# Scores and values of two heads in one matmul, by 32-key groups, in an attention and expert kernel on Trainium2

## The chip, the cores and the metric

The kernel runs on one core of a Trainium2 chip. The metric is device time in microseconds of one execution. Three runs of the kernel before took 649.19, 650.42 and 650.88 us, a median of 650.42. One more execution was taken by the hardware profiler; its own time is in the table below.

## The reference

The kernel computes a windowed attention over q, k and v (batch 8, 8 heads, 576 positions, 64 features, all float32) and feeds the result to a mixture of 8 experts. Of the reference these lines matter:

```python
rel = pos[:, None] - pos[None, :]
mask_plain = (rel >= 0) & (rel < window)
mask_dil = (rel >= 0) & (rel < window * dilation) & (rel % dilation == 0)
masks = np.stack([mask_plain if h < H // 2 else mask_dil for h in range(H)], axis=0)
scores = np.where(masks[None, :, :, :], scores, -1000000000.0)
...
e = fresh_e if s == 0 or local_gate[b, s] < 0.5 else (prev_e if prev_e >= 0 else fresh_e)
...
h = np.maximum(x[b, s] @ w1[e], 0.0)
out[b, s] = p[e] * (h @ w2[e])
```

The window is 32 and the dilation 4. With the positions of a dilated head sorted by their remainder, its mask is a window of at most 32 keys too, so each query sees at most the 32 keys up to its own, in both kinds of heads. The expert of a token is its own best one or, where a gate is open, that of the token before it; then come two matmuls with that expert's weights.

## The kernel before, in words

**Stages.** Attention runs over 32 pairs of heads (`NPB`), each with the 128 features of two heads on the 128 partitions. Its result x goes to DRAM (`xd`). While pairs are worked, the routing of finished tokens (gate logits, the carried choice, places in each expert's list) is cut into steps that run between pairs. Then come units of up to 256 tokens of one expert: rows of `xd` are gathered by index (`xg`, L959 to L960), turned, and multiplied with that expert's weights (L1088, L1183). Weights come as loads of 2 MB (L876) into `raw1` and `raw2`.

**One pair.** `scores(n)` multiplies keys by queries in nine blocks of 64 keys for each head (L342): the weights are the 64 features of one head times 64 keys, so the tile of the array is 64x64 and the two heads lie in different halves of its rows. A score tile has, for each head, 256 columns of queries (`UNITS` part 0) or 320 (part 1), so 512 or 640 columns in all; keys of even and odd blocks lie on the lower and upper 64 partitions. VectorE (DVE) applies the mask (L348: max with -640, then min with the mask), ScalarE (ACT) the exponential (L351). `values(n)` multiplies the probabilities, 64 queries at a time, by 128 keys of values with a column of ones behind them (65 columns, L404); DVE divides by the sum in that column (L408, L409) and writes x. A float32 matmul is two instructions on TensorE (PE): 20 score matmuls are 40, and 18 value matmuls are 36.

**Values in two layouts.** The 128 keys that a block of 64 queries needs begin at even blocks for one half of the queries and at odd ones for the other. The load brings one arrangement; `spread(m)` writes the other with two copies on GpSimd (POOL) for each group m of two pairs: L283 (64x1040) and L284 (64x780).

**Loads and stores.** SyncE (SP) issues all loads and stores of attention: for each m one of keys and queries (1184 KB), one of values (650 KB), and three stores of x. Three buffers of each kind rotate. A DMA of SP raises one of eight semaphores in rotation and waits for the one that was issued eight earlier.

**Order.** The orders of PE and DVE are the program's own (`manual_schedule`). The loop over n has this body: load for m = n // 2 + 2 (n even), transposes of an earlier x (`turn`), scores of n, a slot of routing (`gap`), values of n - 1, spread, more transposes and slots, the store of an earlier x. The orders of POOL, ACT and SP are set by the compiler's scheduler from its own estimates, within the dependences. The steps `early_tokens` (in a slot near n = 28) let the first units' rows be gathered: DVE clears one element of `xg` (L959), POOL issues the gather (L960). POOL also makes the table `what` of each routing group (L628), which PE needs for the sums of the group.

## Time and profile before

| what | value |
|---|---|
| median of three runs | 650.42 us |
| time of the profiled execution | 646.66 us |
| span of the profiled execution, first to last instruction | 644.9 us |
| last x of attention ends | 140.9 us |
| PE busy | 606.5 us (94%) |
| DVE busy | 417.6 us (65%) |
| ACT busy | 176.6 us (27%) |
| POOL busy | 243.6 us (38%) |
| DMA moved | 140.12 MB |

The span is what the views divide; the 1.8 us between it and the execution's time lie outside the first and last instruction. In rows of groups, the columns are line, engine, operation, tile written and tile read, shapes, count, then busy time in us and the mean of one in ns, then the idle time before these instructions with what ended it. In rows of the timeline, the first number is the start and the second the time from the start of the first to the end of the last of so many instructions.

### The profile page before, as it was taken

How to read it: one execution, taken by the hardware profiler on the slowest of the kernel's cores; microseconds unless marked ns; L12 is line 12 of the kernel's file. 1: busy time of each engine (PE TensorE's matmuls, PEld its weight loads, DVE VectorE, ACT ScalarE, POOL GpSimd, SP SyncE). 2: the span in 40 equal slices, each digit the busy share in tenths (PEclk: the TensorE clock that was granted, in tenths of full speed). 3: DMA queues.
4: the chain of work that ended last, by engine and by line, in shares of the span. 5: the costliest groups of instructions: out<-in, count | busy, mean ns of one | idle time of the engine just before them, and what ended most of it. 6: DMA issues, size and time to landing. Idle time of an engine off the chain costs nothing.

```text
span 644.9 us, 15442 instructions
## 1 busy us (share of the span) xinstructions
PE 606.5 (94%) x6350; PEld 532.4 (83%) x6350; DVE 417.6 (65%) x976; ACT 176.6 (27%) x320; POOL 243.6 (38%) x219
## 2 busy tenths in 40 slices
PE   6888988889989999999999999999999999999995
PEld 6776776768878899999598998995979999879984
DVE  3768989989596487672747487628292974473851
ACT  2545444353111232212122222121222211213210
POOL 3322142124003655464685435345544455001011
PEclk8999999999999999999999999999999999999998
DMA  9998989398004689677363665855453767470301
GB/s 346 412 326 292 346 279 299 122 363 319 2 33 156 217 321 354 227 257 250 116 238 108 245 240 205 296 188 193 168 187 151 279 229 260 147 270 37 137 33 42
DMA packets 29744, 140.12 MB, mean 217 GB/s; under 512 B 4892, under 2 KB 15260, under 8 KB 23136
## 3 DMA queue, kind: packets, MB, share of 16 engines
q1 hardware_dynamic: 22096, 119.89, 51.0%
q0 software_dynamic: 7568, 19.15, 8.6%
q8 instruction: 52, 0.85, 0.5%
q14 instruction: 28, 0.23, 0.1%
HBM read 145.31 MB, written 19.14 MB: 255 GB/s over the span
## 4 chain that ended last, share of the span: by engine, by line
PE 71%; DVE 15%; issue 6%; DMA 4%; POOL 2%; SPq 0%; ACT 0%; POOLq 0%; DVEq 0%
PE yp L1183 28%; PE hp L1088 20%; PE pv L404 3%; PE hp L1062 3%; PE yp L1171 3%; PE sc L342 3%; DVE pr L348 2%; PE tp L423 2%; DMA vt<-in_v_dram 2%; DVE x L409 1%; POOL xg L960 1%; PE hp L1049 1%; PE yp L1136 1%; PE hp L1039 1%; DMA out_dram<-y,corner 1%
## 5 line engine op out<-in xcount | busy, mean ns | idle before, releaser
L960 POOL DMA_INDIRECT xg<-xd,at x116 | 131.7, 1136 | 142.8 <-DVE xg L959 117.8
L1098 DVE TENSOR_TENSOR h<-hp,h 128x512 f32<-128x512 f32 x45 | 30.7, 688 | 97.2 <-PE hp L1088 97.2
L1183 PE MATMUL yp<-sum,hc 128*128 128x256 f32 x384 | 88.5, 380 | 0.0
L1088 PE MATMUL hp<-xc,sum 128*128 128x128 f32 x720 | 85.6, 275 | 0.0
L1124 POOL DMA_INDIRECT out_dram<-y,tok x35 | 46.9, 1341 | 96.8 <-DVE y L1198 44.7
L1088 PEld LDWEIGHTS hp<-xc,sum 128*128 128x128 f32 x720 | 82.9, 192 | 0.1
L1183 PEld LDWEIGHTS yp<-sum,hc 128*128 128x128 f32 x384 | 72.8, 190 | 9.9
L1198 DVE SCALAR_TENSOR_TENSOR y<-yp,gate,y 128x256 f32<-128x256 f32 x48 | 23.0, 483 | 63.5 <-issue 34.5
L1183 PE MATMUL yp<-raw,h 128*128 128x256 f32 x256 | 61.2, 382 | 0.0
L351 ACT ACTIVATE pr<-pr 128x512 f32<-128x512 f32 x64 | 43.8, 685 | 60.5 <-DVE pr L348 57.9
L1088 PE MATMUL hp<-xe,raw 128*128 128x128 f32 x480 | 58.9, 276 | 0.7 <-ACT xe L993 0.7
L1088 PEld LDWEIGHTS hp<-xe,raw 128*128 128x128 f32 x480 | 56.4, 192 | 1.8 <-ACT xe L993 1.0
L348 DVE SCALAR_TENSOR_TENSOR pr<-sc,mk 128x512 f32<-128x512 f32 x64 | 45.5, 748 | 15.6 <-PE sc L342 14.1
L1183 PEld LDWEIGHTS yp<-raw,h 128*128 128x128 f32 x256 | 47.4, 190 | 9.1 <-issue 3.3
L404 PE MATMUL pv<-vt,pr 128*64 128x65 f32 x1152 | 44.0, 230 | 9.0 <-issue 4.8
L404 PEld LDWEIGHTS pv<-vt,pr 128*64 128x64 f32 x1152 | 38.7, 142 | 12.2 <-issue 6.6
L1099 ACT ACTIVATE h<-h 128x512 f32<-128x512 f32 x45 | 28.4, 632 | 64.6 <-DVE h L1098 51.1
L1092 ACT COPY h<-hp 128x512 f32<-128x512 f32 x45 | 26.4, 586 | 62.4 <-PE hp L1088 62.4
L342 PE MATMUL sc<-kq 64*64 64x96 f32 (+3 forms) x1280 | 35.4, 248 | 6.7 <-issue 2.9
L342 PEld LDWEIGHTS sc<-kq 64*64 64x64 f32 x1280 | 29.5, 138 | 12.4 <-DVE pr L348 4.4
L283 POOL COPY vt<-vt 64x1040 f32<-64x1040 f32 x16 | 16.8, 1052 | 60.6 <-DMA vt<-in_v_dram 46.6
L1191 ACT ACTIVATE y<-yp,gate 128x256 f32<-128x256 f32 x48 | 22.8, 475 | 61.0 <-PE yp L1183 61.0
(248 smaller groups left out, 956.5 us busy)
## 6 DMA issues: line engine op xcount, KB each, us to landing
raw<-in_w_dram SPq DMA_DIRECT2D x50, 2048.0 KB
kq<-in_qk_dram SPq DMA_DIRECT2D x13, 1184.0 KB
vt<-in_v_dram SPq DMA_DIRECT2D x15, 650.0 KB
xd<-x SPq DMA_DIRECT2D x16, 512.0 KB
kq<-in_qk_dram SPq DMA_DIRECT2D x6, 592.0 KB
xg<-xd,at POOLq DMA_INDIRECT x116, 4.3
xd<-x SPq DMA_DIRECT2D x32, 32.0 KB
vt<-in_v_dram SPq DMA_DIRECT2D x2, 325.0 KB
```

The costliest lines, as they stand in the source:

```text
L342: nc.tensor.matmul(sc[c:c + QB, u, lo - a * QB:hi - a * QB], lhsT=kt[h, WIN + j * QB:WIN + (j + 1) * QB], rhs=qt[h, lo:hi], start=True, st ...
L348: nc.vector.scalar_tensor_tensor(to, sc[:, :, :w], -CEIL, mk[:, at:at + w].unsqueeze(1).to_broadcast([P, 2, w]), Alu.max, Alu.min)
L351: nc.scalar.activation(to, to, Act.Exp, scale=SCALE)
L404: nc.tensor.matmul(pv[half * QB:(half + 1) * QB, k - a], lhsT=pr[:, u, (i - a) * QB:(i - a + 1) * QB], rhs=vt[:, slot(i), u], start=True, ...
L960: nc.gpsimd.indirect_dma_start(out=to, out_offset=None, in_=of, in_offset=bass.IndirectOffsetOnAxis(ap=place, axis=0))
L1088: nc.tensor.matmul(to[:, m], lhsT=a[:, m, kk], rhs=b[:, kk], start=first and m == 0 and kk == 0, stop=(kk == DK // 2 - 1), skip_group_chec ...
L1092: nc.scalar.copy(at((0, 1, 3)[k]), of)
L1098: nc.vector.tensor_tensor(at(k), of, at(k), op=Alu.add)
L1099: nc.scalar.activation(at(k), at(k), Act.Relu)
L1124: nc.gpsimd.indirect_dma_start(out=rows_of_out(), out_offset=bass.IndirectOffsetOnAxis(ap=of_unit(u, "tok", j), axis=0), in_=y, in_offset= ...
L1183: nc.tensor.matmul(to, lhsT=a[:, m], rhs=b[:, m], start=first and m == 0, stop=(m == FK // 2 - 1), skip_group_check=True)
L1198: nc.vector.scalar_tensor_tensor(at(k), of, of_unit(u, "gate", k // 2), at(k), Alu.mult, Alu.add)
```

## The change

Both heads of a pair go through one matmul. Keys and values are laid out so that a column (of keys) or a row (of values) belongs to one head and holds zeros in the other head's place.

- **Scores.** Groups of 32 keys in place of 64, both heads at once: the weights are 128 features by 64 columns, 32 keys of one head and 32 of the other, with zeros at the features of the other head. The keys of a group are read with a stride of 18. Each group meets 64 queries (its own 32 and the next 32), 32 at the edges. A score tile has 256 or 320 columns, 576 for a pair in place of 1152; its partitions hold both heads. 19 matmuls a pair, in 128x64 tiles.
- **Values.** 32 queries by 128 rows (two groups of 32 keys for each of two heads) times 130 columns, of which each row fills the 65 of its head: 16 matmuls in 128x32 tiles, and four with 65 columns for the last block.
- **Zeros** are written once at the start into three buffers of keys and three of values, by DVE, ACT and POOL. The loads fill only the other places: 3 DMAs for keys and queries (1152 KB) and 4 for values (585 KB) for each m, in place of one and one.
- **Spread** is called for each pair: L305 in the changed kernel (64x2x585) and L306 (64x2x520), on POOL, but the second copy of pair 0 on DVE.
- **Room.** The second buffer of keys and the third of values lie in the memory of the first `raw1`, `raw2` and `sum` (a tile called `first`), so the first weight load waits for the last scores and values that read there. Tiles of scores take two banks of PSUM in place of four, and other results six in place of four.

The path for inputs out of range (`scores_exact`), which is not taken here, is changed accordingly. The diff, without it and without the host's new layouts:

```diff
 
-    stage = once
-    room(raw1, 0, "raw1", [P, FK, DK, P])
-    room(raw2, 0, "raw2", [P, FK, D])
-    room(sums, 0, "sum", [P, 4, FK // 2, DK // 2, P])
+    first = once.tile([P, 3, FK * D], F32, name="first")
+    raw1[0] = first[:, 0].rearrange("p (m k f) -> p m k f", m=FK, k=DK)
+    raw2[0] = first[:, 1].rearrange("p (m d) -> p m d", m=FK)
+    sums[0] = first[:, 2].rearrange("p (s m k f) -> p s m k f", s=4, m=FK // 2, k=DK // 2)
...
-    banks = attention.enter_context(tc.tile_pool(name="banks", bufs=4, space=PSUM))
-    twos = attention.enter_context(tc.tile_pool(name="twos", bufs=2, space=PSUM))
+    banks = attention.enter_context(tc.tile_pool(name="banks", bufs=4 if exact else 6, space=PSUM))
+    twos = attention.enter_context(tc.tile_pool(name="twos", bufs=2 if exact else 1, space=PSUM))
...
-    vts = [ins.tile([P, 2 * NT + 1, 4, VW], F32, name=f"vt{k}", bufs=1) for k in range(3)]
-    prs = [work.tile([P, 2, PU], F32, name=f"pr{k}", bufs=1) for k in range(4)]
-    scs = [] if exact else [twos.tile([P, 2, 512], F32, name=f"sc{k}", bufs=1) for k in range(2)]
-    for t in vts:
-        nc.gpsimd.memset(t[QB:, NT + 1], 0.0)
+    kqs, vts = ([ins.tile([P, n], F32, name=f"{name}{k}", bufs=1) if (name, k) not in (("kq", 1), ("vt", 2))
+                 else first.rearrange("p a b -> p (a b)")[:, at:at + n] for k in range(3)]
+                for name, n, at in (("kq", WIN + 6 * S, 0), ("vt", 8 * VN, FK * D)))
+    prs = [work.tile([P, PU], F32, name=f"pr{k}", bufs=1) for k in range(4)]
+    scs = [] if exact else [twos.tile([P, 512], F32, name=f"sc{k}") for k in range(2)]
...
+    def keys_of(m):
+        return kqs[m % 3][:, WIN:WIN + 4 * S].rearrange("p (g u s) -> p g u s", g=2, u=2)
+
+    def queries_of(m):
+        return kqs[m % 3][:, WIN + 4 * S:].rearrange("p (g s) -> p g s", g=2)
+
+    def vals_of(m):
+        return vts[m % 3].rearrange("p (g u s) -> p g u s", g=2, u=2)
+
+    for m in (0, 2, 1):
+        for u in range(2):
+            to = keys_of(m)[u * DH:(u + 1) * DH, :, 1 - u]
+            if m == 1:
+                nc.scalar.mul(to, ones[:DH, 0:1].unsqueeze(2).to_broadcast([DH, 2, S]), 0.0)
+            else:
+                nc.vector.memset(to, 0.0)
+    for m in range(3):
+        nc.gpsimd.memset(vals_of(m)[:, :, :, :VN].rearrange("p g u s -> p (g u) s"), 0.0)
+        nc.gpsimd.memset(vals_of(m)[QB:, :, :, VN:VN + VW], 0.0)
...
     def load(m, what, part=None):
 
-        if (m, what) not in held:
-            held[m, what] = (ins.tile([P, 2, KQ], F32, name="kq") if what == "kq"
-                             else vts[m % 3])
-        t = held[m, what]
-        flat, of = ((t.rearrange("p g f -> p (g f)"), qk) if what == "kq"
-                    else (t[:, :NT + 1].rearrange("p i g e -> p (i g e)"), v))
-        w = KQ if what == "kq" else VHALF
-        a, z = {None: (0, flat.shape[1]), 0: (0, w), 1: (w, flat.shape[1])}[part]
-        nc.sync.dma_start(out=flat[:, a:z], in_=of[m, :, a:z])
-
-    def spread(m):
-
-        t = held[m, "vt"]
-        nc.gpsimd.tensor_copy(t[:QB, NT + 1:], t[:QB, :NT])
-        nc.gpsimd.tensor_copy(t[QB:, NT + 2:], t[QB:, :NT - 1])
+        g = slice(part or 0, 2 if part is None else part + 1)
+        of = qk[m].rearrange("p (r g s) -> p r g s", r=2, g=2)
+        if what == "kq":
+            nc.sync.dma_start(out=queries_of(m)[:, g], in_=of[:, 1, g])
+        for u in range(2):
+            if what == "kq":
+                nc.sync.dma_start(out=keys_of(m)[u * DH:(u + 1) * DH, g, u], in_=of[u * DH:(u + 1) * DH, 0, g])
+                continue
+            for k in range(u * WIN, P, QB):
+                nc.sync.dma_start(out=vals_of(m)[k:k + WIN, g, u, :VN],
+                                  in_=v[m, k:k + WIN].rearrange("p (g s) -> p g s", g=2)[:, g])
+
+    def spread(n):
+
+        t = vals_of(n // 2)[:, n % 2]
+        other = nc.gpsimd if n else nc.vector
+        nc.gpsimd.tensor_copy(t[:QB, :, VN:], t[:QB, :, :VN])
+        other.tensor_copy(t[QB:, :, VN + VW:], t[QB:, :, :VN - VW])
 
     def keys(n):
-        t = held[n // 2, "kq"][:, n % 2]
-        return t[:, :WIN + S], t[:, WIN + S:]
+        return keys_of(n // 2)[:, n % 2], queries_of(n // 2)[:, n % 2]
 
     def vals(n):
-        return held[n // 2, "vt"][:, :, n % 2 * 2:n % 2 * 2 + 2]
+        return vals_of(n // 2)[:, n % 2].rearrange("p u (i e) -> p u i e", e=VW)
...
-    load(1, "vt")
     if not exact:
         nc.sync.dma_start(out=cst, in_=con)
+    load(1, "vt")
     spread(0)
+    spread(1)
...
     def scores(n):
         kt, qt = keys(n)
+        kt = kt.rearrange("p u (k i) -> p i (u k)", i=NH)
...
-            for j in range(max(a - 1, 0), z):
-                lo, hi = spans(j, a, z, n == 0)
-                for u in range(2):
-                    h, c = slice(u * DH, (u + 1) * DH), j % 2 * QB
-                    nc.tensor.matmul(sc[c:c + QB, u, lo - a * QB:hi - a * QB],
-                                     lhsT=kt[h, WIN + j * QB:WIN + (j + 1) * QB], rhs=qt[h, lo:hi], start=True,
-                                     stop=True, tile_position=(u * DH, c), skip_group_check=True)
+            for i in range(max(2 * a - 1, 0), 2 * z):
+                lo, hi = max(i * WIN, a * QB), min((i + 2) * WIN, z * QB)
+                if n == 0 and i == 1:
+                    lo = 0
+                c = i % 2 * QB
+                nc.tensor.matmul(sc[c:c + QB, lo - a * QB:hi - a * QB], lhsT=kt[:, i],
+                                 rhs=qt[:, lo:hi], start=True, stop=True, tile_position=(0, c), skip_group_check=True)
             pr = prs[n % 2 * 2 + part]
-            to = pr[:, :, :w]
-            at = kind * S + a * QB
-            nc.vector.scalar_tensor_tensor(
-                to, sc[:, :, :w], -CEIL,
-                mk[:, at:at + w].unsqueeze(1).to_broadcast([P, 2, w]), Alu.max, Alu.min)
+            to = pr[:, :w]
+            nc.vector.scalar_tensor_tensor(to, sc[:, :w], -CEIL, far[:, a * QB:z * QB] if kind else near[:, :w],
+                                           Alu.max, Alu.min)
...
         for (a, z), pr in zip(UNITS, prob.pop(n)):
             pv = bank([P, z - a, VW], "pv")
-            for c in range(a // 2, -(-z // 2)):
-                for u in range(2):
-                    for i in range(2 * c, min(2 * c + 2, NB)):
-                        half, k = (i % 2, 2 * c + u) if i < NB - 1 else (u, NB - 1)
-                        nc.tensor.matmul(pv[half * QB:(half + 1) * QB, k - a],
-                                         lhsT=pr[:, u, (i - a) * QB:(i - a + 1) * QB], rhs=vt[:, slot(i), u], start=True,
-                                         stop=True, tile_position=(0, half * QB), skip_group_check=True)
+            for i in range(2 * a, 2 * z):
+                p, v_, at = pr[:, (i - 2 * a) * WIN:(i + 1 - 2 * a) * WIN], vt[:, :, i // 2 + (1 - i % 2) * NB], i // 4 * 2
+                for c, k, rhs in ([(i % 4, slice(at - a, at + 2 - a), v_)] if at < NB - 1 else
+                                  [(u * 2 + i % 2, NB - 1 - a, v_[:, u]) for u in range(2)]):
+                    nc.tensor.matmul(pv[c * WIN:(c + 1) * WIN, k], lhsT=p, rhs=rhs, start=True, stop=True,
+                                     tile_position=(0, c * WIN), skip_group_check=True)
...
-        if n % 2 and n // 2 + 1 < NPB // 2:
-            spread(n // 2 + 1)
+        if n + 2 < NPB:
+            spread(n + 2)
```

The compiler's scheduler places POOL's instructions anew. First place, POOL before the change, near the end of attention (`vt` are the values, `xg` the gathered rows, `xd` the stored x, DMAHW and DMASW the semaphores of SP's and of POOL's own DMAs):

```order
L284 COPY vt2_105<-vt2_105 64x780
L283 COPY vt0_103<-vt0_103 64x1040 [waits DMAHW2_49,PE_49]
L284 COPY vt0_103<-vt0_103 64x780
L960 DMA xg_2121<-xd_67,row00_2107 128x256 [waits DMAHW4_49,DMAHW7_49,DVE_49,Pool_49]
L960 DMA xg_2121<-xd_67,row10_2108 128x256 [waits DVE_49]
L960 DMA xg_2214<-xd_67,row00_2107 128x256 [waits DVE_49]
L960 DMA xg_2214<-xd_67,row10_2108 128x256 [waits DVE_49]
```

All copies stand ahead of the four gathers. The same place on POOL after the change (`first` holds the values of pairs 28 and 29, `vt0` those of 30 and 31; L975 is the gather):

```order
L975 DMA xg_2259<-xd_67,row00_2245 128x256 [waits DVE_49,Pool_49]
L975 DMA xg_2259<-xd_67,row10_2246 128x256 [waits DVE_49]
L305 COPY first_77<-first_77 64x2x585 [waits DMAHW7_49,DMAHW1_49,PE_49]
L305 COPY first_77<-first_77 64x2x585 [waits PE_49]
L306 COPY first_77<-first_77 64x2x520 [waits DMAHW0_49,DMAHW2_49,DMASW3_49,DMASW2_49]
L306 COPY first_77<-first_77 64x2x520
L975 DMA xg_2357<-xd_67,row00_2245 128x256 [waits DVE_49,Pool_49]
L975 DMA xg_2357<-xd_67,row10_2246 128x256 [waits DVE_49]
L305 COPY vt0_103<-vt0_103 64x2x585 [waits DMAHW3_49,DMAHW1_49,PE_49]
L305 COPY vt0_103<-vt0_103 64x2x585 [waits PE_49]
L306 COPY vt0_103<-vt0_103 64x2x520 [waits DMAHW2_49,DMAHW4_49,DMASW5_49,DMASW4_49]
L306 COPY vt0_103<-vt0_103 64x2x520
```

The copies of pairs 28 to 31 now stand behind two and behind four gathers, and the L306 of pair 28 and of pair 30 waits for semaphores that the gathers ahead of it raise when they land (DMASW2 and 3, DMASW4 and 5). On PE after the change, the values of pair 28 (`pv`, with `pr` the probabilities):

```order
L420 MATMUL pv_2323<-first_77,pr0_105 32x130 [waits DMAHW1_49,DMAHW0_49,DMAHW2_49,PE_49,DMAHW7_49,Activation_49,Pool_49]
L420 MATMUL pv_2323<-first_77,pr0_105 32x130
L420 MATMUL pv_2323<-first_77,pr0_105 32x130 [waits Pool_49]
L420 MATMUL pv_2323<-first_77,pr0_105 32x130 x5
L420 MATMUL pv_2334<-first_77,pr1_106 32x130 [waits Activation_49]
```

The first of them waits for the pair's L305, the third for its L306; the matmuls of pair 29, 30 and 31 wait for their own L306 in the same way. Second place, POOL before the change, around the first group's `what`, a step that waits for DVE's `is_it`:

```order
L284 COPY vt_103<-vt_103 64x780 [waits Pool_49]
L628 ISA
L628 TENSOR_TENSOR what<-is_it,cst 128x9x56 [waits DVE_49,Pool_49]
L628 TENSOR_TENSOR what<-is_it,gates 128x9x56
L283 COPY vt_104<-vt_104 64x1040 [waits DMAHW1_49,PE_49]
L284 COPY vt_104<-vt_104 64x780 [waits Pool_49]
```

And after the change:

```order
L306 COPY first<-first 64x2x520 [waits Pool_49]
L643 ISA
L643 TENSOR_TENSOR what<-is_it,cst 128x9x56 [waits DVE_49,Pool_49]
L643 TENSOR_TENSOR what<-is_it,gates 128x9x56
L305 COPY vt_103<-vt_103 64x2x585 [waits DMAHW7_49,DMAHW5_49,PE_49]
```

The copies ahead of `what` were those of pairs 18 and 19, and are now those of pairs 16 and 17; the copies of pairs 18 and 19 stand behind it.

73 lines of the change are left out of this document (34 added, 39 removed).

## Prediction

> **What bounds the kernel now.** I first read the page's slices, then the busy time by stage, and then the groups of the first 157 us, in which attention runs (to 140.9 us) and the first expert work follows.
>
> ```profile
> core 0: 644.9 us, clock 0.988
> ...
> PE   6888988889989999999999999999999999999995
> ...
> DVE  3768989989596487672747487628292974473851
> ...
> DMA  9998989398004689677363665855453767470301
> ```
>
> ```profile
> core 0: us, PE busy (x) PEld busy (x) DVE busy (x) ACT busy (x) POOL busy (x), PEclk, DMA share, GB/s
> 10.00:50.00 40.00, 32.93 (x824) 28.48 (x824) 24.62 (x59) 17.48 (x32) 13.20 (x14) 0.91 1.00 372
> 50.00:90.00 40.00, 34.31 (x861) 28.34 (x857) 36.00 (x110) 20.83 (x38) 12.05 (x12) 1.00 0.89 310
> 90.00:127.00 37.00, 32.19 (x738) 27.42 (x736) 34.19 (x107) 16.26 (x30) 8.97 (x9) 1.00 0.68 228
> 127.00:141.00 14.00, 10.75 (x248) 8.96 (x244) 12.90 (x51) 6.71 (x13) 3.96 (x4) 1.00 0.94 329
> ```
>
> From about 157 us on PE is full and the change touches nothing there. What counts is when the last x (pair 31) is written; what follows it is shifted one to one. Attention has three limits. From 10 to 50 us DMA is at 1.00 and PE at 0.82; DVE, at 0.62, has slack. From 50 to 127 us DVE is at 0.90 to 0.92 (it also carries the routing) and PE at 0.86 to 0.87, so PE is close behind. The last 14 us are again DVE's (0.92).
>
> ```profile
> L348 DVE SCALAR_TENSOR_TENSOR pr<-sc,mk 128x512 f32<-128x512 f32 x64 | 45.5, 748 | 15.6 <-PE sc L342 14.1 <-ACT xt L427 1.0 <-ACT xt L429 0.4
> L409 DVE TENSOR_TENSOR x<-pv,rec 128x256 f32<-128x256 f32 x64 | 29.3, 458 | 2.2
> L283 POOL COPY vt<-vt 64x1040 f32<-64x1040 f32 x16 | 16.8, 1052 | 60.6 <-DMA vt<-in_v_dram 46.6 <-PE pv L404 8.6 <-PE sc L342 5.3
> L284 POOL COPY vt<-vt 64x780 f32<-64x780 f32 x16 | 13.8, 864 | 0.9
> L263 POOL MEMSET vt<- 64x260 f32 x3 | 0.8, 309 | 0.3 <-POOLq L1493 0.3
> ```
>
> **DVE's saving.** The mask step takes 512 and 640 columns now (mean 748 ns, two for each pair) and 256 and 320 after. No row has it at the new size. The nearest is x at L409, which also reads PSUM, with 256 and 320 columns: mean 458 ns. That gives 2 x (748 - 458) = 0.58 us for each pair, 18.6 us over 32 pairs at the most. It counts only where DVE is the limit and PE lets it.
>
> **PE's cost.** A pair's chain of scores and values, and a stand-in for the new value shape, stand in the order of time:
>
> ```profile
> 133.73 0.99 PE L342 MATMUL sc<-kq 64*64 64x96 f32 x40
> 134.65 1.27 PE L404 MATMUL pv<-vt,pr 128*64 128x65 f32 x36
> 135.85 0.66 PE L423 MATMUL tp<-cst,x 128*128 128x128 f32 x4
> ...
> 376.27 1.96 PE L1155 MATMUL yp<-raw,h 128*32 128x128 f32 x64
> 378.15 2.05 PE L1088 MATMUL hp<-xe,raw 128*128 128x128 f32 x16
> ```
>
> From start to start, 40 score instructions take 0.92 us (23 ns each, 64x64 tiles) and 36 value instructions 1.20 us (33 ns, 128x64 tiles with 65 columns). After, scores are 38 instructions in 128x64 tiles with at most 64 columns, just the tile of today's values: 38 x 33 = 1.25 us, +0.33; if the column count or the short groups help, down to +0.27. Values are 32 instructions with 130 columns and 8 with 65 in 128x32 tiles. L1155 has such tiles with 128 columns at (378.15 - 376.27) / 64 = 29 ns; so 40 x 29 = 1.16, -0.04. I take +0.25 for each pair. The keys' weights are now read with a stride, which no row shows; I price that at nothing, with a bound of its own among the rivals. [...]
>
> **Sum by stretches.**
>
> *Start, -1.5 us.* Values of pair 0 wait for POOL's copies:
>
> ```profile
> 10.44 1.04 POOL L283 COPY vt<-vt 64x1040 f32<-64x1040 f32 x1 [7.62 <-DMA vt<-in_v_dram]
> 11.54 0.84 POOL L284 COPY vt<-vt 64x780 f32<-64x780 f32 x1
> ...
> 11.53 0.45 PE L404 MATMUL pv<-vt,pr 128*64 128x65 f32 x8 [2.88 <-POOL vt L283]
> ```
>
> Now the copy waits for the whole first load of values until 10.4. After, POOL first clears three buffers of 128x4x585. From the copies, 260 elements more cost 1.04 - 0.84 = 0.20 us, so 2340 cost about 2 us; with the 0.3 us clears and three buffers POOL is free at about 9, and the copy (1170 elements, 1.15) ends by 10.2, against 11.48. The copy of the second half is on DVE. The gain is 1.3 to 1.5; but SP issues 27 DMAs ahead of the loop where it issued 9, so I keep -3 to +1.
>
> *Pairs 2 to 11, +1 us.* DVE's saving is worth little with DVE at 0.62. PE pays 10 x 0.25 = 2.5, partly in its slack; each pair of pairs loads 1737 KB in place of 1834 KB (1152 + 585 against 1184 + 650), which at 372 GB/s is 0.26 us each, -1.3 for five. 2.5 - 1.3, rounded: +1 (-3 to +3). SP issues ten DMAs for two pairs where it issued five, and eight may be open, so it reaches less far ahead: the upper end.
>
> *Pairs 12 to 27, -3.5 us.* DVE gives back at most 16 x 0.58 = 9.3. Some 17 pairs fall into the 77 us from 50 to 127, 4.5 us each; PE had 0.13 of that free, 0.6, and pays 0.25 of it, so the pair can shrink by about 0.35 at most before PE is the limit: 16 x 0.35 = 5.6. Against it stand two costs. First, POOL's `what` of the first routing group:
>
> ```profile
> 79.33 1.03 POOL L628 TENSOR_TENSOR what<-is_it,cst 128x504 f32<-128x504 f32 x1 [8.60 <-DVE rec L408]
> 80.33 1.65 POOL L628 TENSOR_TENSOR what<-is_it,gates 128x504 f32<-128x504 f32 x1
> 81.93 1.04 POOL L283 COPY vt<-vt 64x1040 f32<-64x1040 f32 x1
> ...
> 82.78 1.27 PE L404 MATMUL pv<-vt,pr 128*64 128x65 f32 x36
> ```
>
> Before, the copies behind it were not due for another pair of pairs. In the new order the copies that stand behind it are those of pairs 18 and 19. They end 2 x 1.15 + 1.05 = 3.35 after 81.9, at 85.3, where the values of pair 18 started at 82.78: 2.5 us late, of which I count 1 after the pair's own slack. Second, POOL holds DVE up:
>
> ```profile
> 52.84 1.10 DVE L484 TENSOR_TENSOR eq<-lt,mx 128x72 f32<-128x72 f32 x1
> ...
> 123.63 0.23 DVE L484 TENSOR_TENSOR eq<-lt,mx 128x72 f32<-128x72 f32 x1
> ...
> 52.81 1.05 POOL L283 COPY vt<-vt 64x1040 f32<-64x1040 f32 x1 [6.59 <-DMA vt<-in_v_dram]
> ```
>
> The same step takes 0.87 us more when a copy runs. Copies grow from 16.8 + 13.8 = 30.6 us to 32 x 1.15 + 31 x 1.05, about 69; such meetings grow with them. I count 1 us. [...] So 5.6 - 2 = 3.5; the ends are -9 and 0.
>
> *Tail, +11 us.* This decides. In the new order POOL's copies for pairs 28 to 31 stand behind the first row gathers, and the copy L306 of pair 28 waits until the first two have landed, that of pair 30 until the next two have. Behind the waiting copy on POOL stand the copy of pair 29, the third and fourth gather and the copies of 30 and 31; behind PE's third value matmul of pair 28, which needs that copy, stand all transposes and scores that follow.
>
> ```profile
> 127.21 0.35 SPq L876 DMA_DIRECT2D raw<-in_w_dram  x1
> ...
> 127.65 0.06 DVE L959 MEMSET xg<- 1x1 f32 x2
> ...
> 128.96 1.08 POOL L960 DMA_INDIRECT xg<-xd,row  x1 [9.16 <-issue]
> 130.35 0.98 POOL L960 DMA_INDIRECT xg<-xd,row  x1 [0.31 <-issue]
> ...
> 126.63 0.69 PE L404 MATMUL pv<-vt,pr 128*64 128x65 f32 x16
> ...
> 140.40 0.49 DVE L409 TENSOR_TENSOR x<-pv,rec 128x320 f32<-128x320 f32 x1
> ...
> DMA to landing us min/median/max: 3.0/7.1/8.2
> ```
>
> Counted from the clear of xg at 127.65, pair 28's values started at -1.0 and the last x ended at +13.2. The gathers, behind 2 MB of weights issued at 127.21, land at 130.35 + 7.1 = 137.45, +9.8. After: copy to +10.9, pair 28's values to +12.0, nine transposes and a small matmul to +13.4, scores of pair 30 to +14.7. The clear of the fourth gather follows the mask step of pair 30 on DVE (which starts with half of these scores, at +13.9, and takes 0.9); with POOL's issue about +15.6; landing takes the 3.0 of an empty queue: +18.6. Copy to +19.7, values of 30 to +20.9, transposes to +22.5, values of 31 to +23.6, last x +24.3. So +11.1. If the next 2 MB (raw2, which now also waits for the values of pair 29, since it lies on their buffer) get ahead of the fourth gather, it lands some 5 us later: +16. If the first two wait only 3.0, about +5.5.
>
> Sum: -1.5 + 1 - 3.5 + 11 = **+7 us**. The profiled run of 646.66 us (span 644.9) would become 653.7; it lies 3.8 below the median of the runs, so I forecast 650.42 + 7 = **657.4 us**.
>
> **Rivals.**
> 1. *PE keeps its 23 ns in the scores* (64 columns in place of 96), so DVE's saving is whole in pairs 2 to 27: -26 x 0.58 = -15.1 in place of +1 - 3.5. Then 650.42 - 1.5 - 15.1 + 11 = 644.8, faster. For it: shorter columns. Against: 33 ns in the present 128x64 rows, and DVE's slack up to 50 us. It decides from a score chain of at most about 0.95 us, with no copy late. Chance 0.13.
> 2. *The gathers are quick*: they run ahead of the weights and the tail costs 5.5: 651.9, no change. Against: 8.2 us in the row. Chance 0.10.
> 3. *The change's saving doesn't arrive*: POOL's doubled copies take from DVE what the mask step gives, pairs 12 to 27 give 0, or raw2 holds the fourth gather (+16): 661 to 663. Chance 0.18.
> 4. *The weights of the scores load slowly*: at 46 ns, twice the present, a chain is 1.75 us, PE pays 0.8 for each pair; ten early pairs 8 us, the 16 others 0.25 each (0.8 less the free 0.6), 4: 650.42 - 1.5 + 12 + 11 = 672. [...] Chance 0.05. [...]
>
> The forecast itself has 0.54 (651 to 661). What can be told from no change is 0.3%, 2 us: faster 0.15, same 0.12 (rival 2 and the low edge of the forecast), slower 0.73; faster is rival 1 and 0.02 of the forecast, where its lowest ends meet. The range for 8 in 10 is 644.5 to 664: it takes in rivals 1 to 3 and leaves out rival 4 and the ends that only meet by chance.
>
> **What would show it.** Right: mask steps near 458 ns; the score chain near 1.25 us; PE waiting for POOL's L306 at pairs 28 and 30, some 8 us and 4 us; the last x near 148 us. Wrong: no such waits, because the gathers land within 3 us or the copies don't wait; or a score chain under 1 us with DVE's busy share down by a tenth and pairs closer together. A start of the expert stage before 141 us would refute the sum.

## The result and the profile after

The changed kernel took 689.33 us (median of four runs, 688.77 to 690.8), the kernel before 649.81 us beside it: a ratio of 1.061, interval 1.0586 to 1.0635. The forecast was 657.4 us in a range to 664. The sign was right, the size was not: +40 us where +7 was forecast.

Three points of the profiled executions (spans 644.9 and 686.9 us, so +42.0) divide the difference. The clear of `xg`, from which the tail was counted, came at 149.89 us in place of 127.65: **+22.2**. From there to the end of the last x it took 34.7 us in place of 13.2: **+21.5**. All that follows took 502.3 us in place of 504.0: **-1.7**.

```profile
149.89 0.06 DVE L974 MEMSET xg<- 1x1 f32 x2
...
184.13 0.49 DVE L424 TENSOR_TENSOR x<-pv,rec 128x320 f32<-128x320 f32 x1
```

Busy time by stage:

```profile
core 0: us, PE busy (x) PEld busy (x) DVE busy (x) ACT busy (x) POOL busy (x), PEclk, DMA share, GB/s
10.00:50.00 40.00, 38.19 (x740) 35.83 (x740) 21.42 (x58) 13.02 (x30) 20.13 (x19) 0.96 1.01 268
50.00:90.00 40.00, 39.63 (x739) 36.25 (x738) 24.96 (x82) 14.37 (x34) 17.31 (x16) 1.00 1.02 285
90.00:127.00 37.00, 34.65 (x599) 30.72 (x600) 24.08 (x75) 10.41 (x24) 20.34 (x18) 0.95 0.85 241
127.00:141.00 14.00, 14.00 (x249) 12.13 (x251) 12.27 (x37) 3.87 (x9) 6.32 (x5) 1.00 1.01 273
141.00:180.00 39.00, 25.06 (x393) 22.40 (x385) 15.99 (x71) 6.94 (x16) 12.62 (x12) 0.74 0.47 159
```

PE is now the limit all the way to the tail (0.94 to 1.00; before, 0.82 to 0.87 up to 127 us), with fewer matmuls in each stretch up to 127 us (740 in place of 824 from 10 to 50 us). DVE, the limit before from 50 us on, is at 0.54 to 0.65 up to 127 us: the mask step did get shorter, and nobody uses it. DMA is at 1.01 too, as it was before from 10 to 50 us, but moves 268 GB/s there in place of 372. From 141 to 180 us PE stands a third of the time.

PE around one pair, in order of time:

```profile
25.17 2.50 PE L362 MATMUL sc<-kq 128*64 128x64 f32 x38
27.59 1.22 PE L420 MATMUL pv<-vt,pr 128*32 128x130 f32 x40
28.74 2.49 PE L362 MATMUL sc<-kq 128*64 128x64 f32 x38
```

From start to start the 38 score matmuls take 27.59 - 25.17 = 2.42 us, 64 ns each, where 33 were forecast and 23 stood before. The 40 value matmuls take 1.15 (forecast 1.16). The groups of the page show what is different: the load of weights of a score took 138 ns before and takes 209 now. The first two rows are of the kernel before.

```profile
L342 PE MATMUL sc<-kq 64*64 64x96 f32 (+3 forms) x1280 | 35.4, 248 | 6.7 <-issue 2.9
L342 PEld LDWEIGHTS sc<-kq 64*64 64x64 f32 x1280 | 29.5, 138 | 12.4 <-DVE pr L348 4.4
...
L362 PEld LDWEIGHTS sc<-kq 128*64 128x64 f32 x836 | 52.7, 209 | 8.0 <-DVE pr L366 3.8
L362 PE MATMUL sc<-kq 128*64 128x64 f32 (+1 forms) x836 | 55.2, 283 | 4.4 <-DVE pr L366 3.7
```

The mask step takes, by form, 418 and 491 ns, a mean of 455 where 458 was forecast:

```profile
L366 DVE SCALAR_TENSOR_TENSOR pr<-sc,far 128x320 f32<-128x320 f32 x16 | 7.9, 491 | 13.4 <-PE sc L362 11.6 <-PE last L537 1.8
L366 DVE SCALAR_TENSOR_TENSOR pr<-sc,far 128x256 f32<-128x256 f32 x16 | 6.7, 418 | 10.5 <-PE sc L362 10.5
```

DVE at the start: the copy for pair 0 stands ahead of the first mask and waits for a load. The first mask comes at 11.33 us (before 6.01), the first of pair 2 at 17.85 (15.20). The first two rows are of the kernel before.

```profile
6.01 1.42 DVE L348 SCALAR_TENSOR_TENSOR pr<-sc,mk 128x512 f32<-128x512 f32 x2 [4.72 <-PE sc L342]
15.20 1.58 DVE L348 SCALAR_TENSOR_TENSOR pr<-sc,mk 128x512 f32<-128x512 f32 x2 [0.21 <-PE sc L342]
...
9.77 1.40 DVE L306 COPY vt<-vt 64x1040 f32<-64x1040 f32 x1 [3.39 <-DMA vt<-in_v_dram]
...
11.33 0.82 DVE L366 SCALAR_TENSOR_TENSOR pr<-sc,near 128x256 f32<-128x256 f32 x2
...
17.85 0.42 DVE L366 SCALAR_TENSOR_TENSOR pr<-sc,far 128x256 f32<-128x256 f32 x1 [0.35 <-PE sc L362]
```

The tail on POOL, with the four gathers (L975) and the copies behind them:

```profile
150.81 1.08 POOL L975 DMA_INDIRECT xg<-xd,row  x1 [14.92 <-DVE rec L423]
152.20 0.98 POOL L975 DMA_INDIRECT xg<-xd,row  x1 [0.31 <-DVE pr L366]
153.22 2.26 POOL L305 COPY first<-first 64x1170 f32<-64x1170 f32 x2
159.07 2.06 POOL L306 COPY first<-first 64x1040 f32<-64x1040 f32 x2 [3.59 <-DMA xg<-xd,row]
163.89 0.97 POOL L975 DMA_INDIRECT xg<-xd,row  x1 [2.76 <-DVE xg L974]
168.02 0.95 POOL L975 DMA_INDIRECT xg<-xd,row  x1 [3.15 <-DVE over L542]
169.02 2.26 POOL L305 COPY vt<-vt 64x1170 f32<-64x1170 f32 x2
176.00 2.06 POOL L306 COPY vt<-vt 64x1040 f32<-64x1040 f32 x2 [4.72 <-issue]
```

And PE, which waits for these copies:

```profile
160.18 2.17 PE L420 MATMUL pv<-first,pr 128*32 128x130 f32 x36 [5.11 <-POOL first L306]
...
177.11 2.17 PE L420 MATMUL pv<-vt,pr 128*32 128x130 f32 x36 [5.96 <-POOL vt L306]
```

The L306 of pair 28 starts 9.2 us behind the clear (forecast 9.8), as it should. That of pair 30 starts 26.1 behind it, where 18.6 was forecast: the second weight load `raw2` went out half a microsecond behind the fourth gather, and the copy came 8.0 us after the gather's issue in place of 3.0. That the load held the gather is inferred from these times; no run took it apart.

```profile
168.52 0.36 SPq L891 DMA_DIRECT2D first<-in_w_dram  x1
```

### The profile page after: what moved, and what is told of

Its sections match the earlier page's. It is cut to its first block, busy times and chain, and to the rows that moved or that the text cites. A ratio compares the mean times of both kernels' runs of the same rounds, so it can differ in the third digit from the quotient of the medians.

```text
span 686.9 us, 15820 instructions
## 1 busy us (share of the span) xinstructions
PE 650.7 (95%) x6414; PEld 578.9 (84%) x6414; DVE 412.6 (60%) x981; ACT 164.9 (24%) x322; POOL 289.3 (42%) x253
## 4 chain that ended last, share of the span: by engine, by line
PE 52%; DVE 9%; issue 8%; POOL 4%; DMA 2%; POOLq 0%; DVEq 0%
PE yp L1198 25%; PE hp L1103 16%; PE hp L1077 3%; PE yp L1186 3%; POOL xg L975 2%; PE hp L1054 1%; DMA out_dram<-y,corner 1%; PE hp L1064 1%; DVE first L936 1%; DVE first L933 1%; DMA xg<-xd,row 1%; DVE first L934 1%; PE yp L1151 1%; DVE first L935 0%; PE pv L420 0%
## 5 line engine op out<-in xcount | busy, mean ns | idle before, releaser
L975 POOL DMA_INDIRECT xg<-xd,at x116 | 131.1, 1131 | 141.8 <-DVE xg L974 117.3
L1103 PE MATMUL hp<-xc,first 128*128 128x128 f32 x848 | 101.6, 276 | 1.2 <-DVE xg L974 0.9
L1103 PEld LDWEIGHTS hp<-xc,first 128*128 128x128 f32 x848 | 97.8, 192 | 1.9 <-DVE xg L974 1.3
L1103 PE MATMUL hp<-xe,first 128*128 128x128 f32 x496 | 60.8, 276 | 0.2 <-ACT xe L1008 0.2
L362 PEld LDWEIGHTS sc<-kq 128*64 128x64 f32 x836 | 52.7, 209 | 8.0 <-DVE pr L366 3.8
L362 PE MATMUL sc<-kq 128*64 128x64 f32 (+1 forms) x836 | 55.2, 283 | 4.4 <-DVE pr L366 3.7
L1103 PEld LDWEIGHTS hp<-xe,first 128*128 128x128 f32 x496 | 58.0, 192 | 1.0 <-ACT xe L1008 0.5
L368 ACT ACTIVATE pr<-pr 128x256 f32<-128x256 f32 x64 | 28.3, 444 | 79.1 <-DVE pr L366 76.9
L975 POOL DMA_INDIRECT xg<-xd,row x16 | 17.6, 1103 | 64.3 <-DVE xg L974 25.5
L420 PE MATMUL pv<-vt,pr 128*32 128x130 f32 (+1 forms) x880 | 30.8, 283 | 7.5 <-POOL vt L306 7.5
L305 POOL COPY vt<-vt 64x1170 f32<-64x1170 f32 x22 | 25.6, 1185 | 23.6 <-DMA vt<-in_v_dram 15.2
L420 PEld LDWEIGHTS pv<-vt,pr 128*32 128x32 f32 x880 | 25.8, 116 | 9.9 <-POOL vt L306 8.2
L1198 PE MATMUL yp<-raw,h 128*128 128x256 f32 x128 | 30.7, 382 | 0.0
```

Of the source, the lines that this page charges most:

```text
L305: nc.gpsimd.tensor_copy(t[:QB, :, VN:], t[:QB, :, :VN])
L362: nc.tensor.matmul(sc[c:c + QB, lo - a * QB:hi - a * QB], lhsT=kt[:, i], rhs=qt[:, lo:hi], start=True, stop=True, tile_position=(0, c), sk ...
L368: nc.scalar.activation(to, to, Act.Exp, scale=SCALE)
L420: nc.tensor.matmul(pv[c * WIN:(c + 1) * WIN, k], lhsT=p, rhs=rhs, start=True, stop=True, tile_position=(0, c * WIN), skip_group_check=True)
L975: nc.gpsimd.indirect_dma_start(out=to, out_offset=None, in_=of, in_offset=bass.IndirectOffsetOnAxis(ap=place, axis=0))
L1103: nc.tensor.matmul(to[:, m], lhsT=a[:, m, kk], rhs=b[:, kk], start=first and m == 0 and kk == 0, stop=(kk == DK // 2 - 1), skip_group_chec ...
```

## The experiments

The theory after the result had three parts. S: the step of 18 words in the keys makes the score weights slow to load. D: the loads over 32 or 64 partitions move fewer bytes in the same time. P: the place of POOL's copies costs the tail. The rivals were G (the shape of the tile, not the step, makes the scores slow), and S alone. Each time stands beside runs of the kernel before on the same chip. The traces of all_three, no_zeros and the two runs with few loads come from chips on which the kernel before takes about 665 us and was not traced, so their times within attention are compared with less certainty.

**strides.** The changed kernel with the weights of scores read at steps of 1, 2, 6 and 18 words, by pair in turn; tile and columns stay, other keys are multiplied.

```diff
-        kt = kt.rearrange("p u (k i) -> p i (u k)", i=NH)
+        st = (1, 2, 6, 18)[n % 4]
+        kt = kt.rearrange("p u s -> p (u s)")
...
-                nc.tensor.matmul(..., lhsT=kt[:, i],
+                nc.tensor.matmul(..., lhsT=kt[:, i:i + 63 * st + 1:st],
```

> The changed kernel, but the weights of the score matmuls are read with a step of 1 element in pairs 0, 4, 8 and so on, of 2 in pairs 1, 5, ..., of 6 in pairs 2, 6, ... and of 18, as in the changed kernel, in pairs 3, 7, ...; count, shapes and tiles of the matmuls stay, but apart from step 18 they take other columns of the keys than the computation needs, so only attention's times are read (the expert stage depends on the data). Theory S (the step of the weight reads makes the score chain long): from its start to the start of the next work a chain of 38 takes about 2.45 us at step 18, as measured, and about 1.25 us (33 ns each, the rate of the values before) at step 1; weight loads take 140 ns at step 1 and 209 at 18. Whether 2 and 6 lie with 18 or in between is open. Theory G (the tile, 128 rows by 64 columns with half of the weights zero, makes it long): all four chains take 2.4 to 2.5 us and all weight loads about 209 ns.

Behind it, as behind the other runs with other keys or few loads, the path for inputs out of range ran, so only their attention stage is read. Score chains of four pairs in a row, steps 1, 2, 6 and 18:

```profile
25.85 1.36 PE L363 MATMUL sc<-kq 128*64 128x64 f32 x38
...
28.28 1.42 PE L363 MATMUL sc<-kq 128*64 128x64 f32 x38
...
33.99 2.47 PE L363 MATMUL sc<-kq 128*64 128x64 f32 x38 [0.20 <-issue]
...
37.54 2.50 PE L363 MATMUL sc<-kq 128*64 128x64 f32 x38
```

The same tile with step 1 takes 1.36 us, from start to start 1.29, near the forecast 1.25. S stands, G falls: the whole excess of the chain is the step.

**steps_3_4_5_8.** The same edit, on the kernel of order_fixed (below), with the steps 3, 4, 5 and 8.

> As the run with steps 1, 2, 6 and 18, but with steps 3, 4, 5 and 8 in turn, and with the two edits of order; again other columns of the keys than needed, only attention's score chains are read. Steps 1 and 2 gave about 1.3 us, 6 and 18 about 2.4. If a weight read costs by the 16 bytes that it touches, 3 lies between (about 1.6 to 2.0) and 4, 5 and 8 at 2.4. If it costs by another unit, the jump lies elsewhere: at 8 and not at 4 and 5 (32 bytes).

```profile
29.35 2.07 PE L367 MATMUL sc<-kq 128*64 128x64 f32 x38
...
32.49 2.58 PE L367 MATMUL sc<-kq 128*64 128x64 f32 x38
...
37.28 2.46 PE L367 MATMUL sc<-kq 128*64 128x64 f32 x38
...
40.81 2.60 PE L367 MATMUL sc<-kq 128*64 128x64 f32 x38
```

The price rises between step 2 (1.42 us) and step 4 (16 bytes, 2.58) and stays flat to 18 (2.46 to 2.60). Step 3, with about 2.0 us from start to start, costs half as much again as step 1 here. So the first of the two forecasts came true: by the 32 bytes of the other, steps 4 and 5 would have stayed below 8, and they cost the same. Why a read costs so was not shown.

**before_step9.** The kernel before, with its keys permuted on the host so that each block of 64 is read at a step of 9: the suspected cost put into the old kernel.

```diff
+        kt = kt[:, WIN:].rearrange("p (k j) -> p j k", j=NB)
...
-                                     lhsT=kt[h, WIN + j * QB:WIN + (j + 1) * QB], rhs=qt[h, lo:hi], start=True,
+                                     lhsT=kt[h, j], rhs=qt[h, lo:hi], start=True,
```

> The kernel before, but its keys are put in DRAM in another order, so that the 64 keys of a block lie 9 elements apart, and the score weights are read with a step of 9; 64x64 tiles, all counts and the result as before. Theory S: the weight loads of the scores go from 133 ns to about 200, the chain of 40 from 0.92 us to between 1.3 and 2.5 us, and the time rises by 8 to 40 us over 649.8. Theory G: chain at 0.92 to 1.0 us, time within 2 us of before.

647.84 us against 648.15, ratio 0.9998 (0.9974 to 1.0022): a miss. The page's groups of this kernel show that the cost was there:

```profile
L343 PE MATMUL sc<-kq 64*64 64x96 f32 (+3 forms) x1280 | 50.4, 294 | 2.3 <-issue 1.2
L343 PEld LDWEIGHTS sc<-kq 64*64 64x64 f32 x1280 | 44.2, 213 | 7.7 <-issue 3.1
```

The weight load rose from 138 to 213 ns and PE's score time from 35.4 to 50.4 us, 15 us more, and none of it reached the end, since PE filled its idle time under DVE and DMA (PE 37.79 of 40 us from 50 to 90, before 34.31). A PE cost shows only behind PE's slack. The changed kernel's score chain takes 1.5 us a pair more than before (2.42 for 0.92), three times as much, and outran it.

**before_halves.** The kernel before, each load of keys or values as two DMAs of 64 partitions with the same bytes.

```diff
-        nc.sync.dma_start(out=flat[:, a:z], in_=of[m, :, a:z])
+        for h in range(0, P, QB):
+            nc.sync.dma_start(out=flat[h:h + QB, a:z], in_=of[m, h:h + QB, a:z])
```

> The kernel before, but each load of keys, queries and values is two DMAs of 64 partitions in place of one of 128: same bytes, same packet sizes, result as before. Theory D (a DMA that touches only part of the partitions moves its packets more slowly, and that is why the changed kernel's loads of 2304 and 2340 bytes take some 150 ns where the rate of the other rows would give 100): the packets of 9472 bytes go from a median of 356 ns to above 480, those of 5200 from 200 to above 270, and the stretch from 10 to 50 us moves at most 300 GB/s in place of 372; the time rises by 4 to 15 us over 648. Rival (packets are slow in the changed kernel only because many small ones meet): medians stay at 356 and 200, time within 3 us of before.

690.28 us against 647.35, ratio 1.0633 (1.0586 to 1.0681): this edit alone costs as much as the whole change. The first stage of it:

```profile
10.00:50.00 40.00, 25.19 (x550) 21.81 (x539) 18.51 (x42) 12.55 (x21) 9.41 (x10) 0.81 1.04 248
```

DMA is as busy as before and moves 248 GB/s in place of 372. The records of the packets say the same: in this stage one of 9472 bytes took 356 ns (median) when its DMA reached 128 partitions and 686 when it reached 64, one of 5200 bytes 200 and 364. D stands, and far stronger than expected: with half the partitions a packet takes 1.8 to 1.9 times as long. Why it does was not shown. Not all of the 43 us need come straight from the loads: PE also stood 14 times, 28.8 us in all, at multiples of 256 of its instructions (read there as waits for its own code; how they are seen stands under no_zeros), where the kernel before stood 7 times, 8.1 us. No run takes the two apart.

**order_fixed.** The changed kernel with the copies of pairs 28 to 31 on ACT, away from the gathers, and DVE's copy of pair 0 behind the masks of pair 0.

```diff
+        if n >= NPB - 4:
+            nc.scalar.copy(t[:QB, :, VN:], t[:QB, :, :VN])
+            nc.scalar.copy(t[QB:, :, VN + VW:], t[QB:, :, :VN - VW])
+            return
```

> The changed kernel with two edits of order: both copies of pairs 28 to 31 are on ACT, so that they do not stand behind the gathers on POOL, and DVE's copy of pair 0 stands behind the masks of pair 0 in place of ahead of them. The keys keep their step of 18. Theory P (the gathers' landing holds the copies, and the copy holds the first masks): from DVE's clear of the gathered rows to the last x it takes 15 to 19 us in place of 34.6 (13.2 in the kernel before, and two score chains that are 1.5 us longer), PE waits for no copy there, TensorE's granted clock stays at 1.00 from 141 to 180 us, and the first mask starts at about 8.2 us in place of 11.3; time 668 to 674 us. Rival (the tail is long because PE's score chains and the weights' 2 MB loads are, whatever stands on POOL): clear to last x above 28 us, time above 683 us.

677.22 us against 648.15, ratio 1.0438 (1.0399 to 1.0476): 11 us of the 40 came back. From the clear (152.26 us) to the end of the last x (173.34) it took 21.1 us in place of 34.7; 15 to 19, and a time of 668 to 674 us, had been expected. PE's waits there, 5.11 and 5.96 us before, are these:

```profile
157.20 2.17 PE L424 MATMUL pv<-first,pr 128*32 128x130 f32 x36 [1.50 <-ACT first L306]
...
168.50 1.21 PE L424 MATMUL pv<-vt,pr 128*32 128x130 f32 x36 [0.34 <-ACT vt L306]
```

P stands, and its price was 13.6 us. The first mask moved from 11.33 to 6.56 us, but the first mask of pair 4 came at 29.42 (in the changed kernel 26.43), because POOL's copies for pairs 2 and 3 waited 4.70 us for a load until 21.03: the start was bound by DMA, and removing DVE's wait gave nothing.

**order_step1.** order_fixed with all score weights at step 1 (other keys are multiplied).

> The changed kernel with the two edits of order (copies of pairs 28 to 31 on ACT, DVE's copy of pair 0 behind the masks) and with score weights read with a step of 1 in all pairs; these are other columns of the keys than the computation needs, so only attention's times are read. Theory S with D behind it: the score chain takes about 1.3 us, PE is no longer the limit, and DMA is: at some 8 us of packet time for two pairs the pairs from 2 to 26 follow each other by 3.9 to 4.3 us, and the last x is written at 150 to 158 us (173.3 with the step of 18, 140.9 before the change). Rival, S alone: with the chain short the saving on DVE arrives, pairs follow by 3.4 to 3.7 us on the mean, last x at 141 us or earlier.

The chain fell to 1.36 us, yet the last x ended at 172.1 us where order_fixed had 173.3, outside both forecasts. The clear came 5.8 us earlier (146.50 us for 152.26), but from there the tail took 25.6 us in place of 21.1. The stages show the next limit:

```profile
50.00:90.00 40.00, 37.45 (x841) 30.58 (x837) 30.64 (x95) 15.46 (x37) 20.38 (x19) 1.00 1.04 296
90.00:127.00 37.00, 26.26 (x584) 22.73 (x581) 22.90 (x76) 10.24 (x25) 18.31 (x18) 0.96 1.03 276
```

DMA stays at 1.03 to 1.04 and PE has idle time again (26.26 of 37 us). From pair 2 to pair 26 the first masks follow each other by 4.9 us on the mean, where 3.9 to 4.3 had been forecast: D was priced too low. S alone falls: behind the split loads most of what the step costs stays hidden. The other way round, whole loads with the step of 18, was not run.

**keys_by_act.** Steps of 1 with the right keys: keys and queries come in one DMA of 128 partitions, two copies a pair on ACT (L312, about 0.69 us each) set the keys between zeros; POOL in the program's order, all its copies ahead of the gathers.

```diff
+    def spread_keys(n):
+        for u in range(2):
+            h = slice(u * DH, (u + 1) * DH)
+            nc.scalar.copy(kps[n % 3][h, :, u], keys_of(n // 2)[h, n % 2].rearrange("p (i k) -> p i k", k=WIN))
```

> The changed kernel with: keys and queries loaded as they lie, by one DMA of 128 partitions for two pairs; ACT writes each pair's keys into a zeroed buffer, 32 keys of one head beside 32 of the other, so that the score weights are read with a step of 1; POOL's order is the program's, with all copies ahead of the gathers; DVE's copy of pair 0 behind the masks. Result as before. By theory S, P and D together: score chain about 1.3 us, DMA packet time about 6.6 us for two pairs, no wait for a gather; the saving on DVE then counts where DVE was the limit (about 0.25 us a pair after PE's extra), last x at 134 to 141 us, time 641 to 649 us, below the 648 of before or equal to it. Rival (what the layout itself costs, more copies on POOL that block DVE, ACT's copies ahead of exponentials, zeros at the start, outweighs the saving): last x above 143 us, time above 651 us.

675.22 us against 647.35, ratio 1.0438 (1.0406 to 1.0469): a miss. A new wait took the place of the old ones. ACT, whose order the scheduler sets, does four key copies together behind other work. The values' loads still reached 32 partitions each, and the last x ended at 169.1 us. PE waits for the copies about once in every two pairs (11 waits, 22.4 us, from 20 to 150 us):

```profile
32.85 2.28 PE L370 MATMUL sc<-kq,first 128*64 128x64 f32 x38 [1.87 <-ACT first L312]
...
42.49 1.79 PE L370 MATMUL sc<-kq,first 128*64 128x64 f32 x38 [2.03 <-ACT first L312]
```

**all_three.** keys_by_act with ACT in the program's order too, and the values, zeros included, in one DMA of 128 partitions (1170 KB in place of four DMAs with 585 KB together).

> As the run with keys by ACT, and two things more: values come from DRAM with the zeros in them, one DMA of 128 partitions and 1170 KB for two pairs in place of four of 32 partitions, and ACT too follows the program's order, so that the copies of keys for pair n + 2 stand right behind the exponentials of pair n. Result as before. So all three causes are taken away: the step of 18 (theory S), loads of part of the partitions (theory D), copies behind gathers (theory P). If they are the whole loss: packets of 9 KB at a median near 350 ns, at most 0.5 us of PE waiting for ACT's key copies in a pair, last x at 134 to 142 us (140.9 before, 184.6 changed, 169.2 with keys by ACT), time 642 to 650 us. Rival (the layout as such loses, by 20 per cent more bytes than before, twice the copies on POOL and 1.3 us of copies on ACT for each pair): last x above 145 us, time above 653 us.

674.27 us against 665.55 on this chip (its runs of the kernel before are some 2.5% longer, so the ratio counts): 1.0134 (1.0097 to 1.0171). Of the 6.1% of the change 1.3% is left, about 9 us. The last x ended at 149.2 us (changed kernel 184.6, kernel before 140.9), so this too is a miss: 134 to 142 was forecast, and above 145 is the rival's range. The first stage:

```profile
10.00:50.00 40.00, 33.26 (x791) 29.59 (x791) 20.87 (x57) 27.16 (x54) 25.42 (x23) 0.91 1.03 413
```

413 GB/s at a share of 1.03, where the kernel before moved 372 at 1.00 and the changed kernel 268 at 1.01: the rate is back, and there are more bytes (2322 KB of loads for two pairs against 1834 before).

**all_three_few_loads.** The same kernel without the loads from the fourth group of pairs on.

```diff
-            for part in (0, 1) if m == 2 else (None,):
+            for part in (0, 1) if m == 2 else ():
                 load(m, "kq", part)
...
-        if ahead:
+        if ahead and m < 3:
             load(m, "vt")
```

> The kernel of all_three with the same loads left out. If the bytes of the loads are its limit (DMA share 0.97 to 1.03, 2.9 MB for two pairs) or the code blocks behind them: two pairs shrink from some 7.9 us to 6.5 to 7, PE's waits at multiples of 256 instructions vanish, and the last x ends 12 to 25 us earlier, at about 125 to 137 us. If the remaining 9 us over before lie in the copies on ACT and POOL or in PE's own chains: the last x stays within 6 us of 149.

The last x ended at 139.7 us, 9.5 us earlier; expected were 12 to 25 for the bytes, under 6 for the copies. It lies between the two, nearer to the first. PE's waits at multiples of 256 instructions (11 waits, 10.1 us, in all_three) are gone, as the first theory had it. The loads cost about what was left, by their bytes or by these waits, and even without them the changed scheme reaches only the last x of the kernel before.

**no_zeros.** Another way to 32-key groups: no zeros at all, each head in 64x32 tiles of its own, 76 score and 72 value matmuls a pair, loads of 128 partitions.

```diff
-                nc.tensor.matmul(sc[c:c + QB, lo - a * QB:hi - a * QB], lhsT=kt[:, i],
-                                 rhs=qt[:, lo:hi], ..., tile_position=(0, c), ...)
+                for u in range(2):
+                    h, c = slice(u * DH, (u + 1) * DH), u * QB + i % 2 * WIN
+                    nc.tensor.matmul(sc[c:c + WIN, lo - a * QB:hi - a * QB], lhsT=kt[h, i * WIN:(i + 1) * WIN],
+                                     rhs=qt[h, lo:hi], ..., tile_position=(u * DH, c), ...)
```

> A version that keeps what the change gains on DVE (256 and 320 score columns for both heads) without zeros: each head's 64 features are one row tile of the array, 32 keys its columns (64x32 tiles), so a group of 32 keys is two matmuls, one for each head, that write different partitions of the same columns; values likewise, 64 rows of one head by 65 columns. Keys, queries and values are loaded by one DMA of 128 partitions each (1152 and 585 KB for two pairs), the second layout of the values is written by two copies on POOL and two on ACT for each pair, of 32 partitions, and x leaves in two DMAs of 64 partitions. Order of POOL and ACT as in the program, copies ahead of the gathers. Result as before. Counts for a pair: 76 score instructions in place of 38 (40 before the change), 72 of values in place of 40 (36). If the array runs four of these tiles at once at 64 ns each, 16 ns an instruction, the scores take 1.2 us and the values 1.2 us or less; DVE's saving of 0.58 us then counts from 50 us on, last x at 131 to 139 us where before had 140.9, ratio to before 0.978 to 0.997. Rival: PE issues no faster than the 23 ns of the 64x64 tiles; 148 instructions then take 3.4 us in place of 2.1, PE is the limit again at some 4.6 us a pair, ratio 1.01 to 1.03.

721.69 us against 664.51, ratio 1.0866 (1.0831 to 1.0901): a miss by ten per cent, though each chain is short (72 value matmuls in about 1.2 us, 16 ns each; that the array runs four such tiles at once at 64 ns each was my assumption, and no run shows it). PE in order of time:

```profile
49.23 1.43 PE L401 MATMUL pv<-vt,pr 64*32 64x65 f32 x41 [1.21 <-issue]
50.60 2.18 PE L420 MATMUL tp<-cst,x 128*128 128x128 f32 x9
52.71 1.68 PE L343 MATMUL sc<-kq 64*32 64x64 f32 x76
54.76 1.24 PE L401 MATMUL pv<-vt,pr 64*32 64x65 f32 x72 [0.37 <-issue]
55.81 0.94 PE L343 MATMUL sc<-kq 64*32 64x64 f32 x55
58.33 0.45 PE L343 MATMUL sc<-kq 64*32 64x64 f32 x19 [1.58 <-issue]
```

The waits are "issue" (nothing that the profile shows) and fall in the middle of a chain. Between them lie 41 + 9 + 76 = 126 matmuls, then 72 + 55 = 127. Counted over the records of matmuls, weight loads and the semaphore instructions between them, PE stood after 961, 1217, 1473, 1729, 1985 and so on to 5057 instructions: seventeen waits in a row, each exactly 256 instructions after the one before, 0.3 to 3.2 us long. The queue that the profile's page calls instruction moved packets of 16384 bytes; one ran from 55.98 to 56.99 us, and PE went on at 58.33. Up to the last x there are 28 such waits over 0.2 us, 54.6 us in all, and at each one PE went on 1.2 to 1.6 us after such a packet had ended. From the counts and from these times I take it that PE was waiting for its own code; the profile doesn't name what it waited for. The last x ended at 205.2 us:

```profile
204.73 0.49 DVE L406 TENSOR_TENSOR x<-pv,rec 128x320 f32<-128x320 f32 x1
```

**no_zeros_few_loads.** The same kernel without the loads from the fourth group on, to tell whether the loads lengthen these waits.

> The kernel of no_zeros with the loads of keys, queries and values from the fourth group of pairs on left out, so the buffers keep the first three groups' data. In no_zeros PE ran dry after exactly 256 of its instructions at a time, 17 times in a row, for 1 to 3 us each; a 16 KB packet of the queue called instruction had ended 1.1 to 1.5 us ahead of each restart. Theory C (the code of PE comes in blocks of 256 instructions, each behind the packets of the loads): without the loads the packets come sooner, the waits at multiples of 256 mostly vanish, two pairs take about 6 to 7 us instead of 10.5, and the last x ends some 40 us earlier. Theory F (a block has a fixed price whatever the loads do): the waits stay, every 4.4 to 5 us, and the last x ends at most 10 us earlier. Theory L (SP's order of loads makes PE wait for keys): the waits were never tied to 256; without the loads they vanish too, but the remaining ones would lie anywhere.

The waits stay at nearly every multiple of 256 instructions, mostly 0.6 to 1.8 us each: 33 over 0.2 us up to the last x, 39.7 us in all, each ended 1.2 to 1.6 us after a packet of that queue. DMA has mostly gone:

```profile
50.00:90.00 40.00, 27.82 (x1211) 22.68 (x1204) 19.96 (x70) 22.99 (x46) 8.54 (x14) 1.00 0.26 63
```

From instruction 961 to 5057, sixteen blocks, it took 64.8 us in place of 74.0, work and waits together: 4.05 us a block in place of 4.6. The last x ended at 175.3 us in place of 205.2, 29.9 us earlier, where theory F allowed 10 and theory C forecast some 40. So neither stands whole. Against C, nearly three quarters of the time in these waits stays without the loads; against F, the last x moved by three times its bound. Less time in these waits makes up 14.9 of the 29.9 us; where the other 15 come from was not taken apart (another chip, and a granted clock of 0.96 in place of 0.83 from 20 to 60 us, are among the differences). Theory L, a late load of keys, falls by the count.

## Why the prediction was wrong, point by point

**The step that failed first** is "scores are 38 instructions in 128x64 tiles ..., just the tile of today's values: 38 x 33 = 1.25 us", with the sentence "The keys' weights are now read with a stride, which no row shows; I price that at nothing". With step 1 it is 1.29 us from start to start, so the argument by tiles was right. With the step of 18 it is 2.42: the step is the whole miss of this term. It also made PE the limit up to the tail, where the sum had DMA and then DVE. Rival 4 named this cause, but its bound of 46 ns was a guess of twice the present 23 ns, a factor that no run shows; measured are 64. With step 1 a score matmul takes 34 ns, 1.5 times the 23, so the rows of 33 and 23 ns did price the tile.

**PE's balance.** At +1.5 for the scores and -0.05 for the values, 26 pairs pay 37.7 us. Of these PE could put 17.6 into its idle time before (7.1 + 5.7 + 4.8 in the three stages), which leaves 20.1. Measured from the first mask of pair 2 (+2.65) to the clear (+22.2) are 19.6. The match is closer than the estimate deserves: over just this stretch PE's busy time grew by 32.8 us and its idle time shrank by 13.2. Part of the idle time before were PE's 7 waits at multiples of 256 instructions, 8.1 us up to the last x; the changed kernel has none. So "pairs 2 to 11, +1" and "pairs 12 to 27, -3.5" became about +20, and DVE's saving, right in size (455 ns for 458), was worth nothing.

**The loads.** "Each pair of pairs loads 1737 KB in place of 1834 KB ..., which at 372 GB/s is 0.26 us each, -1.3" counted the bytes and took the rate from DMAs of 128 partitions. The rate fell to 268. This cost lay under PE's and is not a term of its own in the 40 us; order_step1 shows that it was the next limit, and before_halves, where queries are split too, that split loads alone can be as dear as the whole change.

**The start.** "-1.5 us" rested on POOL's copy. The second copy had gone to DVE, ahead of the masks, and waited 3.39 us for its load; the start was 2.65 us later. I had noted that copy and priced no wait for it, nor the work queued behind it on DVE.

**The tail.** The mechanism was right: both waits of PE are there, and the copy of pair 28 came at +9.2 us (forecast +9.8). The forecast said "+11 us" and "+16" for `raw2` ahead of the fourth gather, and measured are +21.5. Three sizes were off: the fourth gather went out at +18.1 in place of +15.6, behind slower scores; it landed 8.0 us later in place of 3.0; and pairs 30 and 31 took 8.6 us in place of 5.7, with the slow score chain and a granted clock of 0.74 in this stage.

**The rivals.** Nothing of rivals 1 and 2 appeared. Rival 4 came true, at more than its price. Of rival 3 the outcome came, the saving didn't arrive, but through PE's slow scores and not shown through POOL's copies; its other half, `raw2` ahead of the fourth gather, fits the times of the tail and was not tested. The range took in rival 3 and left out rival 4 and the two together. The trace of before could not show the step's price, and the honest bound for an operation that no row shows was much wider than 46 ns.

**What stays open.** How the 40 us divide between the step and the split loads can't be said: the step's removal is mostly covered by the loads, and whole loads with the step of 18 were not run. Moving the copies gives 11; all three repairs together give about 31; the last 9 go with the loads, but all_three_few_loads doesn't tell their bytes from PE's waits at multiples of 256 instructions. That those are waits for code is inferred too. In the tail, what held the fourth gather is inferred. No version here beat the kernel before.

## What to carry to other kernels

Before a layout is changed to save one engine's time, price how each operand is then read: the step of a weight read in memory, and the partitions that each DMA reaches, cost more here than the DVE time saved: 1.1 us a pair for the step (2.42 us for 1.29) and 43 us for the whole of before_halves, against 0.59 us a pair on DVE (two mask steps of 455 ns for 748). Where several engines are close to the limit, as PE, DVE and DMA were here, a saving on one is worth at most the slack of the next, and a cost on one can vanish the same way; so a cost put into the old kernel is judged by the group's busy time first. And when a queue's order is left to a scheduler, look for what its waiting instruction now stands ahead of.
